# Attention into a gated feed-forward on one Trainium2 core: the probabilities of two attention units transposed by 64-row halves in one visit, in the first pair stage

## The chip, the cores and the metric

The kernel runs on one core of one Trainium2 chip. The metric is the device time of one execution in microseconds (us). Lower is better. Five engines of the core work side by side, each with an instruction stream of its own: TensorE (PE in the profile, with its weight loads as PEld), VectorE (DVE), ScalarE (ACT), GpSimd (POOL) and SyncE (SP), which issues most transfers.

## The reference

The input is q, k and v of 8 batches, 8 heads, 576 positions and 64 columns a head. Attention is banded: position i sees position j where 0 <= i - j < 64. The attention output, reshaped to 4608 tokens of 512 columns, goes through a gated feed-forward of width 1536. All of it is float32.

```python
scores = np.matmul(q, k.transpose(0, 1, 3, 2)) / np.sqrt(64)
scores = np.where((rel >= 0) & (rel < 64), scores, -1e9)
attn = softmax(scores)                       # with 1e-9 in the denominator
x = (attn @ v) laid out as [4608, 512]
gate = 1.0 / (1.0 + np.exp(-(x @ w_gate)))
val = x @ w_val
out = (gate * val) @ w_out
```

## The kernel before

The 4608 tokens are ten token tiles: two of 384, six of 512, two of 384. An **attention unit** is one token tile and one pair of heads, so a 512-token unit has eight blocks of 64 queries. A block of 64 queries needs 128 keys, and two blocks with one head each fill the 128 partitions, so the probabilities of a 512-token unit are two tiles (`h` = 0, 1) of 128 partitions by four groups of 128 columns. A unit goes through scores (L242), a masked reduction and the exponentials (L275, L290), a division by the row sums (L297 to L305), a transpose of the probabilities on TensorE (L382 or L395) with a copy by ScalarE from PSUM back over the probabilities (L385 or L400), and the product with v (L425), whose result ScalarE copies out (L416).

The first two token tiles are multiplied in the plain way. The other eight are taken in **pair stages** `s` = 1 to 4 of two tiles each. A pair stage multiplies with seven products per 2x2 block product in place of eight. In its first half it has six **rows** `k` = 0 to 5; in a row the seven **products** `n` = 0 to 6 follow each other, each for `m` = 0 (gate) and `m` = 1 (value), so a row is 84 matmuls of 128x512 (L659). A second half of 252 matmuls (tile `y`) multiplies the hidden values with w_out.

Each product adds into a PSUM bank. `PRODUCTS` gives the bank number of `n`: 0, 1, 2, 1, 0, 1, 2. The banks of `m` = 0 have the tags `b10`, `b11`, `b12`, those of `m` = 1 the tags `b00`, `b01`, `b02`; two more banks, tag `a`, serve attention. The results of the products are combined by `combine`. For `n` = 4 nothing is added: the gate's bank (`b10`) is read by ScalarE's tanh (L465, shown as `g<-pr`), and the value's bank (`b00`) is read by VectorE's multiplication with the gate (L470, shown as `h<-g,pr`). Before that multiplication stand on VectorE the sums of product 3 (L669, then L698), from which the gate of product 3 comes.

While pair stage 1 multiplies, attention for stage 2 and the start of stage 3 is worked off in **visits**, one per row from `k` = 1 on, at the row's end (`far_visits`): the products with v of the two units that are in hand (`done`), then the scores of the next two units. The visit of row `k` = 1 only starts units. So in the rows `k` = 2 to 5 of stage 1, and in later rows of stages 2 and 3, two units have to be transposed before the row's end.

Transposing is done in two ways. `stage_b` takes one unit, whole: eight transposes of 128x128, four into each of two banks of tag `a`, and a copy for each bank. `by_halves` takes two units in one go: for each of them 16 transposes of 64 rows, where the upper 64 rows go to one bank and the lower 64 to another, and a copy for each bank. The first unit has the two banks of tag `a`; the second has

```python
def by_halves(units, extra=lambda r, nm: psum(1 + r, 0, nm)):
    for i, (t, p) in enumerate(units):
        pp = [extra(r, f"pp{r}_{t}_{p}") if i else ps_a.tile([P, DM], F32, name=f"pp{r}_{t}_{p}", tag="a")
              for r in range(2)]
```

that is `psum(1, 0)`, tag `b10`, and `psum(2, 0)`, tag `b00`. These are the banks with number 0 of the products.

The order of the work comes from a planner: `put(time, order, function, ...)` collects events, which are sorted by planned time and then emitted. Matmuls and transposes keep the emitted order on TensorE. On the other engines a list scheduler fixes the order at build time, with the emission order as priority. On the chip each engine works in that fixed order. Beside the products stand, in stage 1, sums of weight blocks that are made once: `sums_make` on POOL, `sums_split` (L607 on ScalarE, L610 on VectorE), `wo_sums` (L562 to L570 on VectorE, L569 on ScalarE; planned at fixed times 10, 30, 50, 70 and 90 us after the stage's start) and, in row 5, the splits of the hidden values for the stage's second half, `h_part` (L737, L738).

Of the kernel before, what the change touches and what calls it, by code (L numbers as in the profile page):

```python
# [38 lines left out]
def attn_ffn(ctx: ExitStack, tc: tile.TileContext, qT, kT, vS, vB, w_gate, w_val, w_out, out, outT):  # L39
# [585 lines left out]
    def size(s):  # L625
        return tt(2 * s)
# [99 lines left out]
    def slots_of(s):  # L726
        ns = SLOTS // (2 * size(s))
        spare = list(range(2 * NPR, ns))
        parts = list(range(2 * NPR))
        ring2 = spare + parts  # L730
        return (ring2 * 2 + spare + ring2[-(NI - 2 * ns - len(spare)):])[:NI]
# [36 lines left out]
    def put(tm, o, f, *a):  # L768
        events.append((tm, o, f, a))
# [2 lines left out]
    DPT = DNT / TB  # L772
    NPT = (1.8, 1.1, 1.8)
    NEAR = ((6, 12, 14), (15, 21, 23), (24, 30, 32), (33, 39, 41))
    WHOLE = (2, 4)
    LOAD_AHEAD = 8
    BEFORE, BEHIND = 0, 12

# [18 lines left out]
    def unit(s, n):  # L797
        return 2 * s + n // 2 % 2, n // 4 + n % 2 * 2
# [9 lines left out]
    at, now = {}, 0.0  # L808
# [19 lines left out]
    for i, (kind, t, j) in enumerate(plan):  # L828
        attend(i)
        at[(kind, t, j)] = now  # L830
        if (kind, t, j) == ("up", 0, 0):
            now = -9.9
# [14 lines left out]
        if (kind, t, j) == ("up", 0, 0):  # L847
            now = 0.0
    for i in range(KINDS * NF):
        j, m = divmod(i, KINDS)  # L850
# [43 lines left out]
    GROUPS = [[unit(s, 2 * g + i) for i in range(2)] for s in range(2, NS) for g in range(NP)]  # L894
    AT = [(1, k) for k in range(1, NK)] + [(s, k) for s in range(2, NS - 1) for k in range(NP)]

    def far_visits(v):
        nonlocal now
        units, done = GROUPS[v] if v < len(GROUPS) else [], GROUPS[v - 1] if v else []
        if v == 0:  # L900
            for x in units:
                put(now - 12, 8, load_qk, *x)
        put(now, 6, stage_s, units, done)
        visit = (len(units) + len(done)) / 2
        for i, x in enumerate(units):
            put(now + 0.1, 8, load_v, *x)
            if i:
                put(now + visit + 2.8, 6, far_rest, *x)
            put(now + visit + (4.2, 6.9)[i], 6, stage_n, *x)
        for x in GROUPS[v + 1] if v + 1 < len(GROUPS) else []:  # L910
            put(now + 0.1, 7.5, load_qk, *x)
        now += visit

    for s in range(1, NS):
        PRT = 1.364 if size(s) == BIG else 1.05
        made = []
        for k in range(NK):
            if s == 1:
                for m in range(2):
                    make = (-24 + 6 * m, -29 + 6 * m)[k] if k < 2 else -25 + 8 * m  # L920
                    put(now + make - (6 if k else 4), 7, sums_load, m, k)
                    put(now + make, 7, sums_make, m, k)
                    for i, at_cut in zip((0, 2), (-14 + 2 * m, -10 + 2 * m) if k == 0 else (-13 + 1.5 * m, -5 + 1.5 * m)):
                        put(now + at_cut, 7, sums_split, m, k, i)
                        put(now + at_cut + 4, 7, sums_store, m, k, i)
                for n, d in ((0, -23 if k == 0 else -14), (4, -12 if k == 0 else -2), (5, -9 if k == 0 else -1)):
                    put(now + d, 7.5, w_load, s, k, n)
            for n in range(NPR):
                if s > 1:
                    put(now - 16, 7.5, w_load, s, k, n)  # L930
                v = AT.index((s, k)) if (s, k) in AT else -1
                for m in range(2):
                    put(now, 9, product, s, k, n, m)
                    now += PRT
                    if s > 1 and v > 0 and (n, m) == (5, 0):
                        put(now, 6, by_halves, GROUPS[v - 1])
                        now += 1.3
                if s == 1 and v > 0 and n in WHOLE:
                    put(now, 6, stage_b, *GROUPS[v - 1][WHOLE.index(n)])
                    now += 1.0  # L940
                if v >= 0 and n == NPR - 1:
                    far_visits(v)
            put(now + 0.5, 5.2, h_diff, s, k)
            made.append(now)
        t0, at_down = now, []
        for n in range(NPR):
            if s == NS - 1 and n == NPR - 1:
                for q in range(2):
                    for k in range(NK):
                        if q == 0:  # L950
                            at_down.append(now)
                        put(now, 9, last_product, s, n, k, (q,))
                        now += PRT / 2
                continue
            for k in range(NK):
                at_down.append(now)
                put(now, 9, last_product, s, n, k)
                now += PRT
        of = slots_of(s)
        free = SLOTS // (2 * size(s)) - 2 * NPR  # L960
        for i, tm in enumerate(at_down):
            n, k = divmod(i, NK)
            if i < free:
                when = min(made[k] + 3, t0 + 0.7) if n == 0 else t0 - 6 + 2 * k
            elif i < free + 2 * NPR:
                when = max(t0 - 2 * PRT * (NPR - 1 - (i - free) // 2) + 1, tm - 9)
            else:
                before = max(x for x in range(i) if of[x] == of[i])
                when = max(tm - 8, at_down[before] + 0.1)
            put(when, 5.2, h_part, s, n, k)  # L970
            if i % 2 == 0:
                put(tm - 12, 7.5, wo_load, s, i // 2)
        if s < NS - 1:
            for n in range(NPR):
                for c in range(2):
                    x = 2 * n + c
                    lo, hi = 2 * size(s + 1) * x, 2 * size(s + 1) * (x + 1)
                    last = max(i for i in range(NI) if 2 * size(s) * of[i] < hi and lo < 2 * size(s) * (of[i] + 1))
                    when = max(at_down[last] + 2, at_down[20] + 2.2 * x * PRT / 1.364)
                    put(when, 5.5, x_part, s + 1, n, c)  # L980
                    put(when + 0.5, 5.6, x_rest, s + 1, n, c)
# [12 lines left out]
    for tm, _, f, a in events:  # L994
        if f in (conv_a, conv_b, conv_c):
            with ExitStack() as behind:
# [4 lines left out]
                j, m = divmod(a[0], KINDS)  # L1001
# [62 lines left out]
```

## Time and profile before

| | |
|---|---|
| time, median of 3 runs | 921.94 us (921.76 to 922.63) |
| profiled execution, first to last instruction (span) | 919.5 us |
| median less span | 2.4 us |
| TensorE busy | 907.5 us, 99% of the span |
| VectorE busy | 679.5 us, 74% |
| ScalarE busy | 476.1 us, 52% |
| granted TensorE clock, mean | 1.000 of full speed |

The profile shows one execution. Its span runs from the first to the last instruction, and the 2.4 us between span and median lie outside what its rows show. In the rows below, a line such as "305.71 3.00 PE L659 MATMUL pr<-slots,ws 128*128 128x512 f32 x12" gives the start, the time to the end of the last instruction merged into it, the engine, the line, the operation, the tiles and the count. The starts are measured, while ends of matmuls are modelled and overlap the next start, so times on TensorE are read from start to start.

### The profile page before, as it was taken

What the parts mean: (1) busy time and instruction counts of PE and PEld (TensorE: products, weight loads), DVE (VectorE), ACT (ScalarE), POOL (GpSimd) and SP (SyncE); (2) the same over time, 40 slices, a digit from 0 to 9 for tenths busy, and PEclk for the clock granted to TensorE, in tenths of its full rate; (3) what the DMA queues carried; (4) which work ended last, traced back from release to release, by engine and by line L of the source; (5) the groups of instructions that cost most, each with busy time, mean ns of one, the idle gap of its engine ahead of it and who ended that gap; (6) DMA issues with size and microseconds to landing.
All of it is one profiled execution on the core that took longest, in us unless ns stands there. A gap on an engine that the chain in (4) does not pass through costs nothing.

```text
span 919.5 us, 18434 instructions
## 1 busy us (share of the span) xinstructions
PE 907.5 (99%) x6584; PEld 788.6 (86%) x6584; DVE 679.5 (74%) x1689; ACT 476.1 (52%) x1208; POOL 129.6 (14%) x204
## 2 busy tenths in 40 slices
PE   6999999999999999999999999999999999999998
PEld 5899999888888888888888888888888888999998
DVE  7887878578898899947666698656655986565881
ACT  7867858554466677525554355424442454222550
POOL 4200000087653402001111100001110000000000
PEclk9999999999999999999999999999999999999999
DMA  9899999679989967787676665766755558888783
GB/s 338 313 406 354 359 324 358 203 244 338 345 315 331 336 241 264 253 270 243 236 233 218 206 189 193 263 217 227 228 188 172 202 187 254 270 252 251 256 256 107
DMA packets 92107, 240.02 MB, mean 261 GB/s; under 512 B 9968, under 2 KB 20080, under 8 KB 92016
## 3 DMA queue, kind: packets, MB, share of 16 engines
q1 hardware_dynamic: 91728, 238.62, 76.1%
q8 instruction: 52, 0.85, 0.4%
q14 instruction: 39, 0.32, 0.1%
q10 hardware_dynamic: 288, 0.23, 0.1%
HBM read 186.91 MB, written 51.90 MB: 260 GB/s over the span
## 4 chain that ended last, share of the span: by engine, by line
PE 97%; ACT 2%; DMA 0%; DVE 0%; issue 0%; SPq 0%; DVEq 0%; ACTq 0%
PE pr L659 47%; PE y L659 23%; PE ph L457 11%; PE y L498 6%; PE s L242 3%; PE ob L425 2%; PE pp L382 1%; PE oo L425 1%; PE pp L395 1%; ACT p L290 1%; DMA k<-in_kT_dram 0%; ACT pT L400 0%; DVE p L275 0%; SPq L195 0%; ACT w L171 0%
## 5 line engine op out<-in xcount | busy, mean ns | idle before, releaser
L659 PE MATMUL pr<-slots,wt 128*128 128x512 f32 (+1 forms) x1728 | 373.8, 375 | 0.0
L659 PEld LDWEIGHTS pr<-slots,wt 128*128 128x128 f32 x1728 | 315.3, 188 | 49.3 <-issue 1.7
L659 PE MATMUL y<-slots,wot 128*128 128x512 f32 (+1 forms) x1008 | 215.8, 375 | 0.0
L659 PEld LDWEIGHTS y<-slots,wot 128*128 128x128 f32 x1008 | 185.5, 188 | 29.6 <-issue 0.2
L465 ACT ACTIVATE g<-c 128x512 f32<-128x512 f32 (+1 forms) x72 | 43.6, 606 | 156.8 <-DVE c L698 154.5
L737 ACT CAST slots<-h 128x512 fp32r<-128x512 f32 (+1 forms) x144 | 83.7, 595 | 71.7 <-PE y L659 41.7
L290 ACT ACTIVATE p<-p,mn 128x128 f32<-128x128 f32 x288 | 108.0, 391 | 22.9 <-DVE mn L275 22.8
L738 DVE TENSOR_TENSOR slots<-h,slots 128x512 fp32r<-128x512 f32 (+1 forms) x144 | 92.9, 666 | 19.4 <-ACT slots L737 18.9
L457 PE MATMUL ph<-slots,w 128*128 128x384 f32 x576 | 104.7, 337 | 0.0
L457 PEld LDWEIGHTS ph<-slots,w 128*128 128x128 f32 x576 | 100.1, 188 | 2.1 <-DVE w L172 0.3
L305 POOL TENSOR_TENSOR p<-p,rs 128x384 f32<-128x384 f32 (+1 forms) x47 | 43.5, 946 | 346.9 <-DVE rs L298 330.7
L659 PE MATMUL pr<-slots,ws 128*128 128x512 f32 x288 | 68.3, 391 | 0.0
L669 DVE TENSOR_TENSOR c<-pr,p 128x512 f32<-128x512 f32 (+1 forms) x48 | 31.4, 655 | 45.0 <-PE pr L659 44.9
L275 DVE CUSTOM_DVE_ANT_0 p<-s,m 128x128 f32<-128x128 f32 x284 | 62.5, 285 | 1.6 <-PE s L242 1.6
L659 PEld LDWEIGHTS pr<-slots,ws 128*128 128x128 f32 x288 | 53.8, 188 | 11.0
L470 DVE SCALAR_TENSOR_TENSOR h<-g,c 128x512 f32<-128x512 f32 (+1 forms) x72 | 48.7, 676 | 6.1 <-DVE c L698 0.5
L498 PE MATMUL y<-w,slots 128*128 128x512 f32 x216 | 52.7, 396 | 0.0
L669 DVE TENSOR_TENSOR u<-pr,p 128x512 f32<-128x512 f32 (+1 forms) x48 | 31.1, 654 | 27.6 <-PE pr L659 14.8
L649 ACT CAST slots<-xf 128x512 fp32r<-128x512 f32 (+1 forms) x48 | 27.9, 598 | 40.5 <-PE y L659 31.7
L498 PEld LDWEIGHTS y<-w,slots 128*128 128x128 f32 x216 | 39.8, 188 | 8.8 <-issue 0.7
L698 DVE TENSOR_TENSOR c<-pr,p 128x512 f32<-128x512 f32 (+1 forms) x48 | 31.2, 654 | 21.3 <-PE pr L659 21.1
L290 ACT ACTIVATION_READ_ACCUMULATOR p<-p,mn 128x1 f32 x240 | 45.1, 188 | 0.0
(93 smaller groups left out, 980.7 us busy)
## 6 DMA issues: line engine op xcount, KB each, us to landing
wt<-wd SPq DMA_DIRECT2D x144, 512.0 KB, 4.3
wot<-wod SPq DMA_DIRECT2D x84, 512.0 KB, 4.2
v<-in_vB_dram SPq DMA_DIRECT2D x24, 512.0 KB, 5.5
wd<-ws SPq DMA_DIRECT2D x48, 256.0 KB, 4.5
w32d<-w SPq DMA_DIRECT2D x36, 256.0 KB, 5.4
wd<-w SPq DMA_DIRECT2D x36, 256.0 KB, 6.1
out_dram<-yo SPq DMA_DIRECT2D x30, 256.0 KB, 5.0
k<-in_kT_dram SPq DMA_DIRECT2D x24, 288.0 KB, 6.3
```

The costliest lines, as they stand in the source:

```text
L275: nc.vector.tensor_tensor_reduce(out=pt[:, u, :], in0=sc[u], in1=masks[key], op0=ALU.add, op1=ALU.min, scale=-SCALE, scalar=3.0e38, accum_ ...
L290: exp = nc.scalar.activation(pt[:, u, :], pt[:, u, :], AF.Exp, bias=mn[:, u:u + 1], scale=-1.0, **sums)
L305: eng.tensor_mul(out=pt, in0=pt, in1=rs.unsqueeze(2).broadcast_to([P, up2(t), P]))
L457: pe(nc.tensor.matmul(ph, l, r, start=i == 0 and 0 in parts, stop=i == len(prs) - 1 and NP - 1 in parts))
L465: act = nc.scalar.activation(g, c, AF.Tanh)
L470: nc.vector.scalar_tensor_tensor(out=out, in0=g, scalar=1.0, in1=val, op0=ALU.add, op1=ALU.mult)
L498: pe(nc.tensor.matmul(yb[y], l, r, start=first and n == 0, stop=last and n == 2))
L659: pe(nc.tensor.matmul(ps, l, r, start=first and i == 0, stop=last and i == 2, skip_group_check=not check))
L669: marks["plus"] = nc.vector.tensor_add(out=o, in0=ps, in1=a).ins
L698: nc.vector.tensor_add(out=c, in0=in0, in1=in1)
L737: nc.scalar.copy(h2[:, 0, :], src)
L738: lo = nc.vector.tensor_sub(out=h2[:, 1, :], in0=src, in1=h2[:, 0, :].bitcast(F32))
```

## The change

In pair stage 1 the two visits by `stage_b`, one unit after product `n` = 2 and one after `n` = 4, are gone. In their place the two units are transposed by `by_halves` between the two sixth products of the row, `(n, m)` = (5, 0) and (5, 1), as stages 2 and 3 already do it. The planner's clock goes on by 1.3 for the visit where it went on by twice 1.0.

```diff
-    WHOLE = (2, 4)
...
                 for m in range(2):
                     put(now, 9, product, s, k, n, m)
                     now += PRT
-                    if s > 1 and v > 0 and (n, m) == (5, 0):
+                    if v > 0 and (n, m) == (5, 0):
                         put(now, 6, by_halves, GROUPS[v - 1])
                         now += 1.3
-                if s == 1 and v > 0 and n in WHOLE:
-                    put(now, 6, stage_b, *GROUPS[v - 1][WHOLE.index(n)])
-                    now += 1.0
                 if v >= 0 and n == NPR - 1:
                     far_visits(v)
```

## Rows read from the trace of the kernel before

**Rows 1.** The page: its head, the engines' busy time, the chain that ended last.

```profile
span 919.5 us, 18434 instructions
...
PE 907.5 (99%) x6584; PEld 788.6 (86%) x6584; DVE 679.5 (74%) x1689; ACT 476.1 (52%) x1208; POOL 129.6 (14%) x204
...
PE 97%; ACT 2%; DMA 0%; DVE 0%; issue 0%; SPq 0%; DVEq 0%; ACTq 0%
```

**Rows 2.** Windows: two rows of stage 1, one of stage 2, the start.

```profile
core 0: us, PE busy (x) PEld busy (x) DVE busy (x) ACT busy (x) POOL busy (x), PEclk, DMA share, GB/s
246.60:271.62 25.02, 25.02 (x232) 21.03 (x228) 24.69 (x69) 16.50 (x51) 15.15 (x29) 1.00 0.91 318
296.62:321.61 24.99, 24.99 (x232) 21.03 (x229) 22.50 (x71) 16.17 (x52) 12.30 (x24) 1.00 0.92 339
452.84:477.40 24.56, 24.56 (x248) 20.37 (x244) 16.01 (x58) 13.71 (x46) 4.08 (x4) 1.00 0.70 238
0.00:4.00 4.00, 0.70 (x8) 0.30 (x8) 0.52 (x3) 1.49 (x2) 2.63 (x13) 1.00 0.51 146
```

**Rows 3.** Timeline of PE, row k = 4 of stage 1.

```profile
296.62 3.02 PE L659 MATMUL pr<-slots,wt 128*128 128x512 f32 x12
...
304.92 1.03 PE L395 MATMUL pp<-ident,p 128*128 128x128 f32 x8
305.71 3.00 PE L659 MATMUL pr<-slots,ws 128*128 128x512 f32 x12
...
311.27 1.03 PE L395 MATMUL pp<-ident,p 128*128 128x128 f32 x8
312.06 2.98 PE L659 MATMUL pr<-slots,wt 128*128 128x512 f32 x12
```

**Rows 4.** Timeline of PE, a row of stage 2.

```profile
452.84 15.26 PE L659 MATMUL pr<-slots,wt 128*128 128x512 f32 x66
468.04 1.21 PE L382 MATMUL pp<-ident,p 64*128 64x64 f32 x32
469.18 4.37 PE L659 MATMUL pr<-slots,wt 128*128 128x512 f32 x18
473.48 2.08 PE L425 MATMUL ob<-p,v 128*64 128x64 f32 x64
```

**Rows 5.** Timeline of DVE: the reader of b00 in stage 2, then stage 1, k = 4.

```profile
466.85 0.69 DVE L470 SCALAR_TENSOR_TENSOR h<-g,pr 128x512 f32<-128x512 f32 x1 [0.58 <-PE pr L659]
...
297.19 0.28 DVE L275 CUSTOM_DVE_ANT_0 p<-s,m 128x128 f32<-128x128 f32 x1
...
303.59 0.69 DVE L669 TENSOR_TENSOR u<-pr,p 128x512 f32<-128x512 f32 x1 [0.77 <-ACT p L674]
...
306.01 0.55 DVE L562 TENSOR_TENSOR wb<-wa 128x256 f32<-128x256 f32 x1
...
313.97 0.68 DVE L470 SCALAR_TENSOR_TENSOR h<-g,pr 128x512 f32<-128x512 f32 x1
```

**Rows 6.** Timeline of DVE, stage 1: rows k = 2, 3 and 5.

```profile
262.03 0.68 DVE L470 SCALAR_TENSOR_TENSOR h<-g,pr 128x512 f32<-128x512 f32 x1
...
289.91 0.68 DVE L470 SCALAR_TENSOR_TENSOR h<-g,pr 128x512 f32<-128x512 f32 x1
...
320.86 0.29 DVE L275 CUSTOM_DVE_ANT_0 p<-s,m 128x128 f32<-128x128 f32 x1 [0.39 <-PE s L242]
...
335.71 1.29 DVE L738 TENSOR_TENSOR slots<-h,slots 128x512 fp32r<-128x512 f32 x2
...
341.11 0.68 DVE L470 SCALAR_TENSOR_TENSOR h<-g,pr 128x512 f32<-128x512 f32 x1
```

**Rows 7.** Timeline of ACT: the gates of product 4, and the copies of halves.

```profile
260.10 0.60 ACT L465 ACTIVATE g<-pr 128x512 f32<-128x512 f32 x1 [0.24 <-PE pr L659]
...
287.81 0.58 ACT L465 ACTIVATE g<-pr 128x512 f32<-128x512 f32 x1
...
311.87 0.58 ACT L465 ACTIVATE g<-pr 128x512 f32<-128x512 f32 x1
...
338.17 0.58 ACT L465 ACTIVATE g<-pr 128x512 f32<-128x512 f32 x1
...
469.40 2.03 ACT L385 COPY p<-pp 128x512 f32<-128x512 f32 x4
```

## The prediction

> **What bounds the kernel now.** I read the page first. TensorE is busy for 99% of the span, and the chain that ended last is 97% TensorE [rows 1]. So a microsecond taken out of TensorE's stream is a microsecond of the whole, and so is any microsecond for which TensorE is made to wait.
>
> Next I cut windows at the first product of each row (call that moment T0 of the row) for the rows k = 2 to 5 of stage 1, which the change touches, and for rows of stage 2, which already has the new form. In stage 1 TensorE has no gap: busy 24.99 of 24.99 us. The other thing to see is VectorE: it is busy for 22.5 to 24.7 us of a row of some 25 us in stage 1, and for 16.0 of 24.56 us in stage 2 [rows 2]. VectorE is nearly full exactly where the change is made, and it isn't where the same visit already runs.
>
> Last I read the timelines of TensorE, VectorE and ScalarE in these rows, for what the new visit would have to wait for.
>
> **The change part by part.**
>
> *The transposes themselves.* From the start of eight whole transposes to the start of the next product is 305.71 - 304.92 = 0.79 us, and 312.06 - 311.27 = 0.79 us for the second unit: 1.58 us a row [rows 3]. The two units by halves take 469.18 - 468.04 = 1.14 us [rows 4]. That is 0.44 us less a row, and the windows say the same: a row of stage 1 takes 24.99 to 25.02 us and one of stage 2 takes 24.56 us with the same matmuls otherwise [rows 2]. Four rows: **-1.76 us**. Weight loads double in number, but that is already in the 1.14 us.
>
> By the Trainium skill, TensorEngine Tiling (Array Packing), section Theoretical Speedup, a contraction of 64 rows may gain up to two times; as an estimate by that page the two units would take half of the 1.58 us, 0.79 us, and the four rows would save 3.2 us. The trace does not agree, with 1.14 us.
>
> *What is hidden.* ScalarE makes four copies of 128x512 a row before and after. No transfer is issued by either form. The planner's clock runs 0.7 us less a row, so later events move against the fixed times of the output-weight sums by at most 2.8 us; TensorE waits for none of these now, and I cost this at nothing.
>
> *The probabilities.* The units are needed later than before (both at about T0 + 15 us; before, the first was needed at T0 + 8.3 us), so the division by the row sums gets more room. There is nothing to gain there, since TensorE does not wait for it.
>
> *The banks.* Here the price lies. Whole transposes use the two banks of tag a alone. The halves of the second unit go to b10 and b00. These hold product 4 of the same row, whose last matmul ends one product before the visit. b10 is free when ScalarE has made the gate (L465, `g<-pr`), b00 when VectorE has multiplied (L470, `h<-g,pr`). Until then the second unit's transposes wait, and on TensorE's queue everything stands behind them: product (5, 1), product 6, the products with v, the next scores.
>
> When does TensorE come there? In stage 2 the visit starts 468.04 - 452.84 = 15.20 us after T0 [rows 4], and I take the same for stage 1, as the products are the same. The first unit is half of the 1.14 us: the second unit's banks are wanted at T0 + 15.77 us.
>
> When is b00 read out? In stage 2 L470 ends at 466.85 + 0.69 = 467.54, T0 + 14.70 us: 1.07 us to spare [rows 5]. In stage 1 VectorE is late. L470 ends (start plus duration) [rows 5, 6], with T0 from the windows [rows 2]:
> - k = 2: 262.71 - 246.60 = 16.11 us after T0, so 0.34 us late;
> - k = 3: 290.59 - 271.62 = 18.97 us, 3.20 us late;
> - k = 4: 314.65 - 296.62 = 18.03 us, 2.26 us late;
> - k = 5: 341.79 - 321.61 = 20.18 us, 4.41 us late.
>
> Together 10.21 us. Would these moments stay? VectorE's work before L470 in a row begins with the reductions of the new scores, which follow TensorE, and then runs nearly without a gap. In row 4 the only larger one is 0.77 us, for a copy on ScalarE [rows 5]; it is in no part a wait for a product of that row. So an earlier product 4 doesn't bring L470 forward: what stands before it does, among it the sums of output weights (L562 and on) in rows 3 and 4 and the splits for the second half (L738) in row 5 [rows 5, 6]. All this was emitted before product 4, so I expect the list scheduler to leave it there.
>
> Two corrections. In row 4 the reductions began at T0 + 0.57 us, VectorE being behind from row 3; in row 5 they waited for the scores and began at T0 - 0.75 us [rows 5, 6]. If TensorE stands still for 3 us in row 3, VectorE catches up there, and row 4 is late by 1.32 us less: 0.94 us. Sum 8.89 us, the **upper bound** of this term. The other way: product 4 is now planned 1 us earlier in its row, so in rows 3 and 5 one VectorE instruction or so may fall behind L470. Two of these start 0.6 us apart (two in 1.29 us) [rows 6]; that makes 1.2 us less: **7.7 us**, the value I take.
>
> The **lower bound**: L470 can't come ahead of its gate. If it followed the gate at once, it would end 0.68 us after the gates' ends at 260.70, 288.39, 312.45 and 338.75 [rows 7], so 14.78, 17.45, 16.51 and 17.82 us after T0. Against 15.77 that is 0, 1.68, 0.74 and 2.05 us late; with row 4's catching up, 3.7 us.
>
> *The sum.* -1.76 + 7.7 = +5.9 us on the profiled span of 919.5 us, so 925.4 us. With the 2.4 us by which the median stands above the span: 921.94 + 5.9 = **927.9 us**. With the bounds of this term: 923.9 us (3.7) to 929.1 us (8.89).
>
> **The rivals.**
>
> *No wait, only the shorter transposes.* The scheduler puts L470 of product 4 early enough that b00 is free by T0 + 15.8 us in all four rows. Then 921.94 - 1.76 = 920.2 us. For it: stage 2 runs so, with 1.07 us to spare. Against it: three of the four gates end later than T0 + 15.8 us as well [rows 7], and these wait on sums that VectorE makes late. L470 would have to come forward by 2.3 to 4.4 us in three rows.
>
> *A smaller wait, bound by the gate.* L470 follows its gate closely: 923.9 us, as worked out.
>
> *The copies come late too.* The second unit's two copies must be done before the products with v, because these write b10 and b00 again. In stage 2 the four copies end at 471.43 and the products with v begin at 473.48 [rows 4, 7], 2.05 us to spare. In stage 1 the second unit ends later, and if its copies stood behind the gate of product 6, they would come after 12 matmuls (two thirds of 4.30 us, 2.87), VectorE's sum (0.7), the gate (0.6) and themselves (1.0): 5.2 us against the 4.30 us that 18 matmuls take [rows 4]. That is 0.9 us a row, 3.6 us in all: 931.5 us. Against it: the copies are emitted ahead of that gate.
>
> *The clock falls in a long wait.* In row 5 TensorE would stand for some 4 us, in row 3 for 3. If the granted clock went to its lower level, 1.2 for 2.4 GHz, the 18 matmuls behind would take 4.30 us more, once or twice: 932 to 937 us. Against it, weakly: TensorE was idle for most of the first 4 us, and the granted clock there is 1.00, as it is everywhere in this trace [rows 2]. The Trainium skill (TensorE: Matmul & The Clock Gate, section Why this matters for your kernels) warns of idle gaps between bursts of matmuls, after which the clock is halved; no stretch of this trace shows such a fall.
>
> That the change doesn't do what it says I exclude: TensorE keeps the emitted order.
>
> **How the numbers follow.** The wait on b00 in about its present size, 925.5 to 930.5 us: 0.58. No wait, 920.2 us: 0.13. The wait bound by the gate, around 923.9 us: 0.13. The copies late as well: 0.09. The clock: 0.07. The forecast is that of the first, 927.9 us. The range of 922.8 to 932 us leaves out the case without a wait and that of the clock, 0.20 together. What a measurement of this kernel can tell from no change is about 0.2%, 1.84 us. The case without a wait lies at -1.74 us, just inside: 0.05 of it counts as faster and 0.08 as the same. The one bound by the gate lies just beyond on the other side: 0.06 same, 0.07 slower. So faster 0.05, same 0.14, slower 0.81.
>
> **What would show it.** In rows 2 to 5 of stage 1, 32 transposes from L382 between 66 and 18 matmuls of L659. After the first 16 of them an idle time of TensorE released by VectorE's L470: up to 0.3 us in row 2, some 3 us in row 3, 1 us in row 4 and 4 us in row 5. The rows last 24.56 us plus that wait. VectorE's idle time grows behind it, as it catches up. Stages 2 to 4 keep their lengths. The prediction is wrong if the rows of stage 1 fall to 24.6 us, if the idle time is put down to ScalarE's copies or lies before the products with v, or if the granted clock falls below 1.00.

## The result and the profile after

The changed kernel takes **930.19 us** (median of 4 runs, 929.52 to 934.27) against 922.26 us for the kernel before on the same chip: a ratio of 1.0095 over all runs (the two medians alone give 1.0086), 95% interval 1.0074 to 1.0116. The profiled execution of the changed kernel has a span of 927.7 us, 8.2 us more than before [rows 1].

The page of the changed kernel (head, busy time, the chain that ended last):

```profile
span 927.7 us, 18552 instructions
...
PE 908.6 (98%) x6648; PEld 786.5 (85%) x6648; DVE 680.4 (73%) x1689; ACT 477.7 (51%) x1208; POOL 132.3 (14%) x204
...
PE 63%; DVE 2%; ACT 1%; issue 0%; DVEq 0%
```

The chain no longer stays on TensorE [rows 1]: VectorE stands in it with 2%, some 19 us, most of it in row 5, where one VectorE instruction after the other set the time. ScalarE's 1% is mostly the exponentials (L290) at the start of row 5, whose results VectorE then divides. The shares add up to two thirds of the span; the earlier third isn't in it.

Windows of the changed kernel, the four rows k = 2 to 5 of stage 1, each from its first product to the next row's:

```profile
core 0: us, PE busy (x) PEld busy (x) DVE busy (x) ACT busy (x) POOL busy (x), PEclk, DMA share, GB/s
246.78:272.48 25.70, 25.05 (x248) 20.21 (x245) 25.33 (x70) 16.65 (x52) 16.05 (x28) 1.00 0.90 308
272.48:298.30 25.82, 25.03 (x248) 20.42 (x245) 23.13 (x71) 16.33 (x51) 13.26 (x23) 1.00 0.93 339
298.30:324.26 25.96, 24.85 (x248) 20.50 (x245) 21.79 (x66) 16.62 (x52) 9.05 (x16) 1.00 0.84 312
324.26:354.85 30.59, 26.83 (x249) 21.65 (x245) 27.01 (x69) 19.22 (x56) 0.00 (x0) 0.94 0.60 201
```

Together 108.07 us, against 100.00 before (246.60 to 346.60): 8.07 of the 8.2 us. Row 5 alone has grown by 5.6 us, and its granted clock is 0.94.

The timeline of PE in the changed kernel, at the places where it waits:

```profile
256.08 3.02 PE L659 MATMUL pr<-slots,ws 128*128 128x512 f32 x12 [0.65 <-DVE u L669]
...
263.11 1.21 PE L382 MATMUL pp<-ident,p 64*128 64x64 f32 x32
264.25 1.65 PE L659 MATMUL pr<-slots,wt 128*128 128x512 f32 x6
...
287.91 0.77 PE L382 MATMUL pp<-ident,p 64*128 64x64 f32 x17
289.46 0.71 PE L382 MATMUL pp<-ident,p 64*128 64x64 f32 x15 [0.79 <-DVE h L470]
290.10 1.63 PE L659 MATMUL pr<-slots,wt 128*128 128x512 f32 x6
...
313.49 0.77 PE L382 MATMUL pp<-ident,p 64*128 64x64 f32 x17
315.37 0.71 PE L382 MATMUL pp<-ident,p 64*128 64x64 f32 x15 [1.11 <-DVE h L470]
316.01 1.66 PE L659 MATMUL pr<-slots,wt 128*128 128x512 f32 x6
...
338.50 1.66 PE L659 MATMUL pr<-slots,wt 128*128 128x512 f32 x6 [0.34 <-DVE c L669]
340.09 0.71 PE L382 MATMUL pp<-ident,p 64*128 64x64 f32 x16
341.45 0.28 PE L382 MATMUL pp<-ident,p 64*128 64x64 f32 x1 [0.65 <-ACT g L465]
344.50 1.11 PE L382 MATMUL pp<-ident,p 64*128 64x64 f32 x15 [2.77 <-DVE h L470]
345.54 2.71 PE L659 MATMUL pr<-slots,wt 128*128 128x512 f32 x6
```

The wait has the place that was named: after 16 or 17 of 32 transposes, where the second unit goes to b10 and b00. The seventeenth writes b10 and may go ahead, the eighteenth needs b00 and waits for L470; in row 5 the seventeenth waits as well, for the gate. In row 2 the 32 go through in 1.14 us, as in stage 2 [rows 4]. But there is a second kind of wait: product 3 waits for L669 in row 2 (tile u), product 5 in row 5 (tile c).

Windows of the changed kernel around the long wait in row 5:

```profile
342.00:344.00 2.00, 0.00 (x0) 0.00 (x0) 2.00 (x5) 0.99 (x2) 0.00 (x0) 1.00 0.00 0
...
345.00:346.00 1.00, 1.00 (x12) 0.88 (x9) 0.74 (x2) 0.49 (x2) 0.00 (x0) 0.50 0.00 0
346.00:347.00 1.00, 1.00 (x4) 0.71 (x4) 0.00 (x0) 0.68 (x2) 0.00 (x0) 0.50 0.00 0
347.00:348.00 1.00, 1.00 (x4) 0.81 (x3) 0.13 (x1) 0.62 (x1) 0.00 (x0) 0.57 0.00 0
348.00:349.00 1.00, 1.00 (x6) 0.80 (x5) 1.00 (x2) 0.00 (x0) 0.00 (x0) 1.00 0.00 0
```

The column behind POOL is the granted clock: the lower level (0.50, 1.2 GHz) after an idle time in which TensorE did nothing, and the full one again from 348 us on. The six matmuls from 345.54 on take 2.55 us to the next start (348.09), where six in row 4 take 1.50 (316.01 to 317.51).

From start to start, what each row takes beyond the 24.56 us of a row of stage 2 (in a row of stage 2: 15.20 us to the visit, 1.14 in it, 8.22 from there to the next row):

| row | beyond | before the visit (products 3 and 5) | in the visit | behind it |
|---|---|---|---|---|
| 2 | 1.14 | 1.13 | 0.00 | 0.01 |
| 3 | 1.26 | 0.23 | 1.05 | -0.02 |
| 4 | 1.40 | -0.01 | 1.38 | 0.03 |
| 5 | 6.03 | 0.63 | 4.31 | 1.09 |
| sum | 9.83 | 1.98 | 6.74 | 1.11 |

With the 1.76 us that shorter transposes save: 9.83 - 1.76 = 8.07 us.

### The profile page after: what moved, and what is told of

It reads as the page before. It is cut to its first block, busy times and chain, and to the rows that moved or that the text cites. A ratio compares the mean times of both kernels' runs of the same rounds, so it can differ in the third digit from the quotient of the medians.

```text
span 927.7 us, 18552 instructions
## 1 busy us (share of the span) xinstructions
PE 908.6 (98%) x6648; PEld 786.5 (85%) x6648; DVE 680.4 (73%) x1689; ACT 477.7 (51%) x1208; POOL 132.3 (14%) x204
## 4 chain that ended last, share of the span: by engine, by line
PE 63%; DVE 2%; ACT 1%; issue 0%; DVEq 0%
PE pr L659 35%; PE y L659 23%; PE ob L425 2%; PE s L242 2%; PE pp L382 1%; ACT p L290 0%; DVE slots L738 0%; DVE p L275 0%; DVE h L470 0%; DVE c L698 0%; DVE h L632 0%; DVE c L669 0%; DVE p L305 0%; DVE th L635 0%; DVE h L638 0%
## 5 line engine op out<-in xcount | busy, mean ns | idle before, releaser
L290 ACT ACTIVATE p<-p,mn 128x128 f32<-128x128 f32 x288 | 108.1, 391 | 19.7 <-DVE mn L275 19.7
L738 DVE TENSOR_TENSOR slots<-h,slots 128x512 fp32r<-128x512 f32 (+1 forms) x144 | 93.3, 668 | 21.9 <-ACT slots L737 21.3
L669 DVE TENSOR_TENSOR c<-pr,p 128x512 f32<-128x512 f32 (+1 forms) x48 | 31.4, 654 | 44.8 <-PE pr L659 44.8
L470 DVE SCALAR_TENSOR_TENSOR h<-g,c 128x512 f32<-128x512 f32 (+1 forms) x72 | 48.8, 677 | 5.8
L669 DVE TENSOR_TENSOR u<-pr,p 128x512 f32<-128x512 f32 (+1 forms) x48 | 31.1, 654 | 27.7 <-PE pr L659 14.8
L290 ACT ACTIVATION_READ_ACCUMULATOR p<-p,mn 128x1 f32 x240 | 45.6, 190 | 0.0
```

What stands on the lines that cost most here:

```text
L290: exp = nc.scalar.activation(pt[:, u, :], pt[:, u, :], AF.Exp, bias=mn[:, u:u + 1], scale=-1.0, **sums)
L470: nc.vector.scalar_tensor_tensor(out=out, in0=g, scalar=1.0, in1=val, op0=ALU.add, op1=ALU.mult)
L669: marks["plus"] = nc.vector.tensor_add(out=o, in0=ps, in1=a).ins
L738: lo = nc.vector.tensor_sub(out=h2[:, 1, :], in0=src, in1=h2[:, 0, :].bitcast(F32))
```

## The experiments

The theory at this point: the second unit waits for the reader of b00, and that reader is late because VectorE's queue is full before it. Rivals: the halves themselves cost more in stage 1, the place is bad by itself, or the wait has another cause (ScalarE, the order).

### Halves at the old places

```diff
-                    if v > 0 and (n, m) == (5, 0):
+                    if s > 1 and v > 0 and (n, m) == (5, 0):
...
+                if s == 1 and v > 0 and n in (2, 4):
+                    put(now, 6, by_halves, [GROUPS[v - 1][n // 2 - 1]])
+                    now += 0.65
```

> Each unit is transposed by halves alone, at the old places (after products 2 and 4), on the two banks of tag a; banks b10 and b00 are left to the products. Theory (the new time is a wait for the reader of b00, and the halves themselves are cheaper): no wait in rows 2 to 5, rows of about 24.56 us, so 4 x 0.44 = 1.76 us less than before: about 920.5 us. Rival (64-row transposes cost more in stage 1, where VectorE and ScalarE are fuller): 922 us or more, rows above 25.0 us.

Measured: 921.79 us, ratio 0.9998 (0.9989 to 1.0007): neither 920.5 nor slower. TensorE's timeline in row 4 of this kernel:

```profile
298.05 3.02 PE L659 MATMUL pr<-slots,wt 128*128 128x512 f32 x12
...
306.44 0.71 PE L382 MATMUL pp<-ident,p 64*128 64x64 f32 x16
307.08 3.02 PE L659 MATMUL pr<-slots,ws 128*128 128x512 f32 x12
...
312.75 0.71 PE L382 MATMUL pp<-ident,p 64*128 64x64 f32 x16
313.39 3.02 PE L659 MATMUL pr<-slots,wt 128*128 128x512 f32 x12
...
322.98 3.02 PE L659 MATMUL pr<-slots,wt 128*128 128x512 f32 x12
```

No wait is listed for TensorE in these rows, so the halves don't cost the 8 us. But the row takes 24.93 us and not 24.56. Two visits of 16 halves take 0.64 us each, 1.28 together where one visit of 32 takes 1.14, and the 84 matmuls take 19.72 us (24.93 less 1.28 and less 3.93 from the products with v to the row's end), 0.23 more than with one visit (24.56 - 1.14 - 3.93 in the next run). With two whole visits at the same places the 84 matmuls took 19.49 us too (row 4 before: 24.99 - 1.58 - 3.92). So a second visit by halves has a price of its own, 0.37 us here, and the saving holds only when two units share one visit. By the Trainium skill, TensorEngine Tiling (Array Packing), section Key Properties, changing the tiling mode drains the engine; the 0.23 us in the matmuls agree with that. Rows 2, 3 and 5 took 25.25, 25.32 and 25.17 us: matmuls of product 3 or 5 stop there until L669 has ended, in waits too short to be listed (in row 3 L669 ends at 283.46 us and the matmuls go on at 283.52).

### VectorE's other work put behind the reader

```diff
-    for k, tm in enumerate((-20, 10, 30, 50, 70, 90)):
+    for k, tm in enumerate((-20, 10, 30, 52.5, 74.5, 97)):
...
     def h_part(s, n, k):
-        with tc.issue_after(marks["T2", s]) if n > 2 and s == NS - 1 else nullcontext():
+        after = marks["T2", s] if n > 2 and s == NS - 1 else marks.get(("b00", 1, NK - 1)) if s == 1 else None
+        with tc.issue_after(after) if after else nullcontext():
...
```

Here `marks["b00", s, k]` is the row's L470 of product 4, and row 5's splits are planned behind it.

> The changed kernel, but VectorE's other work in the rows is put behind the reader of b00: the output-weight sums are planned after product 4 of rows 2, 3 and 4, and in row 5 the splits for the second half stand behind L470 of product 4. Theory (L470 is late because of what stands before it on VectorE): no wait for L470 in any row, no fall of the granted clock, 920.5 to 922.5 us; what remains above 920.5 is waiting of product 3 for bank b01 in row 2 (0.65 us in the changed kernel) and splits that come late in the second half. Rival (L470 is late for another reason, its gate or product 4 itself, or the place is bad by itself): 927 us or more, the waits stay.

Measured: 931.07 us, ratio 1.0098 (1.0084 to 1.0112). The time missed what the theory expected, and the rows hit it. Windows of rows 2 to 5, then TensorE's timeline in row 5 and in the second half, and L470 in row 5:

```profile
246.57:272.05 25.48, 25.36 (x249) 20.14 (x245) 24.84 (x69) 16.66 (x52) 15.36 (x28) 1.00 0.93 324
272.05:296.61 24.56, 24.56 (x249) 20.37 (x245) 22.34 (x65) 16.17 (x50) 13.11 (x23) 1.00 0.94 343
296.61:321.17 24.56, 24.56 (x249) 20.37 (x245) 22.50 (x71) 16.52 (x52) 9.22 (x16) 1.00 0.89 310
321.17:345.73 24.56, 24.56 (x249) 20.38 (x245) 21.26 (x59) 17.13 (x53) 0.00 (x0) 1.00 0.78 276
```

```profile
336.36 1.21 PE L382 MATMUL pp<-ident,p 64*128 64x64 f32 x32
...
364.06 8.49 PE L659 MATMUL y<-slots,wot 128*128 128x512 f32 x29 [2.85 <-DVE slots L741]
373.77 0.49 PE L659 MATMUL y<-slots,wot 128*128 128x512 f32 x1 [1.23 <-ACT slots L740]
376.09 38.01 PE L659 MATMUL y<-slots,wot 128*128 128x512 f32 x155 [1.82 <-DVE slots L741]
```

```profile
335.20 0.69 DVE L470 SCALAR_TENSOR_TENSOR h<-g,pr 128x512 f32<-128x512 f32 x1 [0.61 <-PE pr L659]
```

(L741 is L738 in this file's numbering.) No visit waits, and rows 3 to 5 take exactly a row of stage 2. In rows 3 to 5 L470 ends 14.7 us after T0, as in stage 2, and in row 5 it is now L470 that waits for TensorE. This is the shown part of the theory: with the sums and splits behind it on VectorE, the reader is in time, and the visit at the new place then saves 0.44 us a row. But the splits put off in row 5 were late for the second half, where TensorE waited 5.9 us and the granted clock fell twice to 0.50. The work has to be done somewhere in a stretch in which VectorE is full; only the place of the wait changed.

### Row 5 without the splits

```diff
+            lo = None
+            if s > 1 or n > 2 or n * NK + k < 3 or (n, k) == (1, NK - 1):
+                lo = nc.vector.tensor_sub(out=h2[:, 1, :], in0=src, in1=h2[:, 0, :].bitcast(F32))
```

> The changed kernel without the low halves of the hidden values that row 5 of stage 1 splits (L738, 14 VectorE instructions of products 0 to 2 of the second half; the second half then multiplies old values there, so part of the output is not computed). Theory (in row 5 the reader of b00 is late by the splits before it on VectorE): L470 comes about 5 us earlier after the row's start, row 5 loses its wait (4.3 us with the shorter-clock part), the wait of product 5 (0.6) and the slower matmuls behind (1.1): 930.2 - 6.0 = 924 us, rows 2 to 4 as in the changed kernel. Rival (row 5 is late for another reason, as after the move of the division to POOL): 928 us or more.

Measured: 924.19 us, ratio 1.0024 (1.0015 to 1.0033). The timelines of PE and DVE in row 5 (T0 at 324.30):

```profile
339.49 1.21 PE L382 MATMUL pp<-ident,p 64*128 64x64 f32 x32
...
348.86 11.41 PE L659 MATMUL y<-slots,wot 128*128 128x512 f32 x49
```

```profile
338.34 0.69 DVE L470 SCALAR_TENSOR_TENSOR h<-g,pr 128x512 f32<-128x512 f32 x1
```

L470 ends 14.73 us after T0, and the row takes 24.56 us (324.30 to 348.86): the wait of the visit, that of product 5 and the slow matmuls are gone together, 6.0 us. In row 5 the cause is shown: the splits before L470 on VectorE. ScalarE's exponentials stand where they stood, so they alone don't make it late.

### Whole transposes at the new place

```diff
+    def stage_b(t, p, second=0):
...
+            pp = blocks(psum(1 + h, 0, f"pp{h}_{t}_{p}"), t) if second else bank(t, p, f"p{h}", f"pp{h}_{t}_{p}")
...
-                        put(now, 6, by_halves, GROUPS[v - 1])
+                        if s > 1:
+                            put(now, 6, by_halves, GROUPS[v - 1])
+                        else:
+                            for i, x in enumerate(GROUPS[v - 1]):
+                                put(now, 6, stage_b, *x, i)
```

> In stage 1 both units are transposed whole, but at the new place between the sixth products, the second unit into b10 and b00. Theory (place and banks cost, not the halves): b00 is wanted 0.6 us later than with halves (8 whole transposes 0.79 us, then 4 more 0.40 us), so waits released by L470 of about 0.5 us in rows 3 and 4 and 3 to 4 us in row 5, and 0.44 us more for the transposes in each row: 928 to 931 us. Rival (the halves are what costs): about 922 us, no wait.

Measured: 929.26 us in one run. TensorE's timeline, rows 4 and 5:

```profile
315.49 0.66 PE L395 MATMUL pp<-ident,p 128*128 128x128 f32 x4 [0.94 <-DVE h L470]
...
344.37 0.66 PE L395 MATMUL pp<-ident,p 128*128 128x128 f32 x4 [2.39 <-DVE h L470]
```

The last four transposes, those into b00, wait for the same instruction. So the place with its banks costs, not the halves.

### The second unit on the banks of tag a

```diff
-                        put(now, 6, by_halves, GROUPS[v - 1])
+                        if s > 1:
+                            put(now, 6, by_halves, GROUPS[v - 1])
+                        else:
+                            put(now, 6, by_halves, GROUPS[v - 1][:1])
+                            put(now, 6, by_halves, GROUPS[v - 1][1:])
```

> The changed kernel, but in stage 1 the second unit uses the two banks of tag a again, after the first. Theory: no wait for L470 at all; in its place the second unit waits for ScalarE's copies of the first, 1 to 1.5 us in rows 2 to 4 and some 2 us in row 5: 926 to 929 us. Rival (the wait is not the bank's): waits released by L470 stay, 929.5 us or more.

Measured: 930.05 us in one run, above the range. TensorE's timeline in row 2:

```profile
265.10 0.27 PE L382 MATMUL pp<-ident,p 64*128 64x64 f32 x1 [1.10 <-ACT p L385]
265.58 0.71 PE L382 MATMUL pp<-ident,p 64*128 64x64 f32 x15 [0.22 <-ACT p L385]
```

No wait for L470 is left; two waits a row for ScalarE's copies stand in its place, 4.6 us listed over the four rows. The granted clock fell in row 2 (0.50 in the window 268 to 270), which was not expected. Two units in one visit want four banks, and with both choices tried the second pair was still being read.

### One product later

```diff
-                    if v > 0 and (n, m) == (5, 0):
+                    if v > 0 and (n, m) == ((5, 0) if s > 1 else (5, 1)):
```

> The changed kernel with stage 1's visit one product later, behind (5, 1). Theory (b00's reader decides, at a fixed time after the row's start): b00 is wanted 1.36 us later, so no wait in rows 2 to 4 (0.8 and 1.1 us in the changed kernel) and 2 us in place of 3.4 in row 5: 925 to 927.5 us. Rival (the wait follows the visit, for instance because of the copies): as the changed kernel, 929.5 us or more; copies that come too late would show as waits before the products with v.

Measured: 924.26 us in one run. TensorE's timeline, rows 4 and 5:

```profile
314.41 0.71 PE L382 MATMUL pp<-ident,p 64*128 64x64 f32 x15 [0.16 <-DVE h L470]
...
342.13 0.71 PE L382 MATMUL pp<-ident,p 64*128 64x64 f32 x15 [1.24 <-DVE h L470]
```

No visit waits in rows 2 and 3; one waits 0.16 us in row 4 and one 1.24 us in row 5: the later the visit, the shorter the wait, as a reader at a fixed time after the row's start wants it. In row 5 the visit came later than planned, since product 5 waited for L669 twice (0.35 and 0.75 us). No wait stands before the products with v, so the copies are in time. The clock stays at 1.00 in row 5, which the theory had not counted on; that is part of why the kernel came out faster than its range. In this one run it is the better of the two places, and still 2.3 us above the kernel before.

### The division moved to POOL

```diff
-        eng = nc.vector if 2 <= t < 6 or (t, p, h) == (1, NP - 1, 1) else nc.gpsimd
+        eng = nc.vector if 2 <= t < 4 or (t, p, h) == (1, NP - 1, 1) else nc.gpsimd
```

Three kernels with this edit: the changed one, the changed one with the visit one product later, and the kernel before as control.

> The changed kernel with the division of stage 2's probabilities by the row sums (4 instructions a row of stage 1, about 0.65 us each) moved from VectorE to POOL, which is idle in row 5 and half idle in rows 3 and 4. Theory (VectorE is full, and L470 is late by what stands before it): the first two of the four stood before a wait for ScalarE and give nothing, the other two bring L470 forward by 1.3 to 1.5 us, so no wait in rows 3 and 4 and 2 us in place of 3.4 in row 5, with less or no fall of the clock: 925 to 927 us. Rival (the order or the place, not VectorE's load): 929.5 us or more.

> The same, with stage 1's visit one product later, behind (5, 1). Theory: b00 is read out in time in rows 2 to 4, at most 0.6 us of wait in row 5, rows of 24.6 to 24.8 us: 921 to 922.5 us, the first form with the halves as stage 2 has them that is no slower than before. Rival: 924 us as with the later place alone.

> Control: the kernel before, with the same division moved to POOL. VectorE's load costs the kernel before nothing, since the whole transposes never wait for it: within 0.2% of 922 us. Rival (freeing VectorE is a gain by itself, or POOL's slower division comes late): a change of more than 0.2%.

Measured: 930.72 us (ratio 1.0095, 1.0081 to 1.0109), 925.28 us (1.0037, 1.0024 to 1.0049) and 923.69 us (1.0018, 1.0009 to 1.0027). The first two missed; the control lies at the edge of what was expected. In the first, row 5's L470 ends 20.25 us after T0, as without the edit (20.18). The timelines of POOL and DVE there (the second up to 335.6 us):

```profile
332.21 2.97 POOL L305 TENSOR_TENSOR p<-p,rs 128x512 f32<-128x512 f32 x2 [1.53 <-PE pr L659]
```

```profile
333.35 0.93 DVE L632 TENSOR_TENSOR h<-h 128x512 f32<-128x512 f32 x1
334.20 1.52 DVE L738 TENSOR_TENSOR slots<-h,slots 128x512 fp32r<-128x512 f32 x1
```

While POOL divides, one L632 takes 0.93 us and one split 1.52, where two splits alone take 1.29 together [rows 6]. From start to start these two instructions lose 1.1 us (0.85 and 1.45 in place of 0.60 each), nearly as much as the 1.2 us that the two divisions had taken. So this run says nothing against VectorE's load as the cause; in row 5 it did not lower it. In the control two short waits for POOL's division (0.6 us together) stand before whole transposes.

### Row 5 as before, and rows 3 and 4 alone

```diff
-                    if v > 0 and (n, m) == (5, 0):
+                    if (s > 1 or k < NK - 1) and v > 0 and (n, m) == (5, 0):
...
+                if s == 1 and k == NK - 1 and n in (2, 4):
+                    put(now, 6, stage_b, *GROUPS[v - 1][n // 2 - 1])
```

with the sums at 52.5, 74.5 and 97; in the second kernel the new visit is in `k in (3, 4)`, the old form in `k in (2, 5)`, and the sums are at 50, 74.5 and 97.

> The changed kernel with the output-weight sums planned behind product 4 (as in the run that put VectorE's work behind the reader), and with row 5 transposed whole at the old places; the splits for the second half stay where they were. Theory: rows 3 and 4 take 24.56 us, row 2 some 25.5 (product 3 waits for bank b01), row 5 25.0, and nothing is late in the second half: 921 to 922 us, so the whole of the change's loss sits in the meeting of the new visit with VectorE's queue, most of it in row 5. Rival (the new place costs also where VectorE is not in the way): 924 us or more.

> What the runs so far point to as best: the new visit in rows 3 and 4 of stage 1 alone, with the output-weight sums of these two rows planned behind product 4; rows 2 and 5 as before. Rows 3 and 4 of 24.56 to 24.8 us in place of 25.0, rows 2 and 5 of 25.0: 0.4 to 0.9 us less than before, 921.1 to 921.6 us, at the limit of what can be told. Rival (VectorE is full, and work moved in one row comes back in the next): 922 us or more.

Measured: 922.53 us (1.0008, 0.9999 to 1.0017) and 922.07 us (0.9999, 0.9990 to 1.0008). TensorE's timeline in row 3 of the second:

```profile
281.08 1.66 PE L659 MATMUL pr<-slots,ws 128*128 128x512 f32 x6 [0.22 <-DVE u L669]
```

and in row 2 of the first, which has the visit at the new place there:

```profile
255.77 3.02 PE L659 MATMUL pr<-slots,ws 128*128 128x512 f32 x12 [0.60 <-DVE u L669]
```

The second kernel's rows take 25.26, 25.54, 24.56 and 25.00 us: row 4 gains 0.43 us and row 3 loses 0.54, where product 3 waits for L669. In the first kernel row 3 missed its 24.56 us for the same reason, with 25.59. No visit waits for L470 in either. Where the old form stays, in row 2 of the second kernel and in row 5 of both, no wait of product 3 or 5 is listed. Without row 5 the loss is all but gone in both kernels, as the theory wanted, but no mixture beat the kernel before. Nothing tried is faster than it.

## Why the prediction was right, point by point

**Shorter transposes, -1.76 us: right.** Where nothing waits, rows of the new form take 24.56 us (three rows of the run with VectorE's work put behind, one without the splits). It holds for two units in one visit; two visits give 0.37 of the 0.44 us back. The estimate by the full factor of two was too large: 1.58 us became 1.14, a factor of 1.39.

**The wait for b00, 7.7 us: right in place, releaser and cause; the size was 6.7, of which 0.4 is the clock's.** The visit came 15.2 to 16.3 us after T0, where 15.20 from stage 2 had been taken for every row. Timelines of DVE in the changed kernel, the readers of b00 in rows 2 to 5:

```profile
262.53 0.68 DVE L470 SCALAR_TENSOR_TENSOR h<-g,pr 128x512 f32<-128x512 f32 x1
...
288.73 0.67 DVE L470 SCALAR_TENSOR_TENSOR h<-g,pr 128x512 f32<-128x512 f32 x1
...
314.64 0.67 DVE L470 SCALAR_TENSOR_TENSOR h<-g,pr 128x512 f32<-128x512 f32 x1
...
343.76 0.68 DVE L470 SCALAR_TENSOR_TENSOR h<-g,pr 128x512 f32<-128x512 f32 x1
```

L470 ended 16.43, 16.92, 17.01 and 20.18 us after T0 (before: 16.11, 18.97, 18.03, 20.18). Rows 4 and 5 came nearly as worked out: row 4 caught up by 1.0 us (I had 1.32), and row 5 stayed where it was. Row 3 was mis-sized: I let L470 come 0.6 us earlier, and it came 2.05 earlier, 0.5 of it because VectorE began the row less behind (0.80 us after T0, 1.30 before). The rest is the order there: in the changed kernel the first output-weight sum (L562) stands behind L669 of product 3, and one of the two L570 falls behind L470. By the planner's code this follows from its clock running 0.7 us less a row; no run tried it alone. I had costed that shift of the planner's clock at nothing. In row 5 I had taken off 0.6 us for the same reason, and nothing of it came.

That the term came out near 7.7 is in part luck. With the measured ends of L470 and the prediction's T0 + 15.77 the four rows give 0.66, 1.15, 1.24 and 4.41 us, 7.5 together, where it had 0.34, 2.60, 0.94 and 3.81: row 3 was 1.45 too large, the others 1.2 too small.

**What the prediction left out: the banks with number 1, 2.0 us.** The old visits stood before products 3 and 5, and those two write banks b11 and b01 again, which VectorE (L669) reads out after products 1 and 3. With each visit went 0.79 us of TensorE's time that had covered this reading. In row 3, where no wait is listed, L669 ends at 282.18 us and product 3 goes on at 282.24. The rows with the old form in the last two kernels, which list no such wait, show that the old places did cover it. "There is nothing to gain there" was said of the probabilities; that the old places hid something I did not look for. The 2.0 us would not all come back if this wait went: in rows 2 and 5 it only let the visit come later, towards an L470 that ended at the same time in row 5 before and after (T0 + 20.18). As an estimate, row 2 would gain 1.13 - 0.66 us, row 3 0.23 and row 5 nothing, some 0.7 us.

**The clock, a rival at 0.07: it came beside the forecast, at a third of its price.** After 2.77 us without work the granted clock was 0.50 for about 3 us: 1.1 us on the matmuls behind and 0.4 on the last transposes, where the rival had 4.3. A granted clock below 1.00 stands in the prediction's own list of signs that it is wrong. On this point it was: it had left the clock out of its sum, because the first 4 us of the trace, mostly idle, showed no fall. The Trainium skill (TensorE: Matmul & The Clock Gate, section Why this matters for your kernels) warns of idle gaps between bursts of matmuls; the trace agrees, with 0.50 behind the gap of 2.77 us. When it falls is not settled. It did not after waits of 1.11, 1.24 and 1.42 us. It did after 2.39, 2.71, 2.77 and 2.85, and twice after two shorter ones with little work between: 1.10 and 0.22 us with one transpose between, 1.23 and 1.82 us with one matmul between. In six of the thirteen traces it also fell 17.5 to 19.2 us after the start, behind waits of at most 0.82 us; row 2 of stage 1 begins no later in these six. The executions of the changed kernel with 930.77 and 934.27 us have a mean granted clock of 0.995, the other two 0.998. How much of their spread is the clock's stays open.

**The sum.** -1.76 + 6.7 + 2.0 + 1.1 = 8.1 us, against -1.76 + 7.7 = 5.9 forecast. Two terms that were missing weigh more than the one that was too large. The mechanism that was named is the largest term, and the range held; but it was meant to leave the clock's case out, and nothing in it stood for the wait before products 3 and 5.

**The other rivals.** No wait at all was wrong in three of four rows and right in row 2, there because product 3 had waited first: L470 ended 16.43 us after T0, later than T0 + 15.77. The copies are in time wherever b10 and b00 are used. A wait bound by the gate shows for one transpose in row 5 (0.65 us), and the next one waited on for L470.

## What to carry to other kernels

An operation that runs well in one stage brings its banks with it: before moving it, read for each buffer it takes who reads it last in the *new* stage, and when that reader ends after the row's start. Look also at what the operation hid at its old place, since the time it took there may have covered another reader. And where an engine is full over a whole stretch, putting its work in another order moves the wait and does not remove it.

## What the runs showed of the hardware

While POOL ran two 128x512 multiplications, two of VectorE's 128x512 instructions on data in SBUF took 0.93 and 1.52 us in place of 0.68. The two multiplications took 2.97 us in place of the 2.04 of the pair before them (at 328.64 us). Here work handed to an idle engine was paid for on the full one.
